# Windowed attention and a convolutional feed-forward on one core: weight decoding ahead of the convolution in steps 16 to 24

## The chip, the cores and the metric

One core of a Trainium2 chip runs the whole kernel. The metric is the device time of one execution in microseconds (us), 464.05 us as the median of 3 runs before the change (463.93 to 464.62). Each engine runs its own instructions strictly in order: TensorE (PE) multiplies, VectorE (DVE) and GpSimd (POOL) do elementwise work, ScalarE (ACT) does activations and copies, SyncE (SP) issues most transfers. They meet through semaphores.

## The reference

Attention over 4 batches, 8 heads, 768 positions, head width 64; a query sees 8 global keys and the 96 keys up to its own position, with a slope per head on the distance. Its output, 768 rows of 512 per batch, goes through a feed-forward block with double precision weights, of which the kernel gets the raw 64-bit words.

```python
scores = scale * q @ k.T + bias            # bias = -slope * distance, -1e9 outside the window
a = exp(scores - max(scores)); a = a / (sum(a) + 1e-9)
x = (a @ v) as (batch, 768, 512)
h = maximum(x @ w_in, 0)                   # 512 -> 1024
conv = sum over k in 0..2 of conv_w[k] * h shifted by k - 1 along the positions
out = (h * 1 / (1 + exp(-conv))) @ w_out   # 1024 -> 512
```

## The kernel before, in words

A job is a pair of heads over half a batch (384 queries): 32 jobs of 3 steps each, 96 steps of 128 queries. Step s runs `scores(s)` on TensorE (L385 for the first nine jobs, L395 later), `maxima(s)` on VectorE (L412, two instructions for two heads), `exps(s)` on ScalarE (L426), and, one or two steps late, the rest of the earlier steps: `normalise(s - 1)` takes the reciprocal of the row sums on VectorE (L438) and scales one head on GpSimd (L444) and one on ScalarE (L442); `transposes(s - 2)` (TensorE, L452) and `evict(s - 2)` (ScalarE, L457) turn the probabilities; at a job's end `values` multiplies by v (L473), and `mixed_high` (ScalarE, L485) and `mixed_low` (VectorE, L489) split the result into two float32r planes.

The feed-forward of one half batch (12 steps) is a queue of small items that `fill` works off between the steps of the next half batch. `mm1` multiplies by w_in in three parts for each of 8 blocks f (L507) and ends with a ReLU on ScalarE (L517), which also frees the PSUM bank; up to step 26 there is one such bank, so block f + 1 can't begin before the ReLU of block f. `conv` takes the middle tap on ScalarE (L555, later on GpSimd, L557) and the outer two on VectorE (L558, L559), both on what L555 wrote. For each pair of blocks follow a tanh on ScalarE (`gate`, L577) and a check for saturation (`saturated`, L588). `split` (L610, L612, L613) makes the gated planes and `mm2` multiplies by w_out (L622).

The weights must be made float32 planes. Piece by piece (16 of 128x512; w4_1 is piece 4, half 1), SP loads the words (L307), VectorE puts sign, exponent and mantissa together in three instructions (L316, L318, L320), GpSimd rounds to the high plane (L325), VectorE subtracts for the low one (L331). These wait as chores, and `work("dve", budget)` issues them, in their order, until the budget of its step is used up. A piece that is finished (L320) frees the load four pieces later.

From job 9 on (step 27) q and k are split too, into qh, ql, kk: GpSimd copies (L137, L138), VectorE subtracts (L141, L142), and kk's raw tile has one buffer, so its next load follows the subtraction.

The first 25 steps (s below `HAND`) are laid out by hand: each engine's instructions run in the order in which the program's lines issue them. From step 25 on a scheduler orders each engine's instructions by its own model of the time, starting from where the hand-laid part left the engines. So an edit to the hand-laid steps also changes orders behind them.

In a hand-laid step VectorE's part is: maxima(s), the reciprocal of step s - 1, at a job's end the split of its values, then what `fill` issues (the outer taps of a convolution, in five of the steps from 17 on: 17, 19, 20, 22, 23), then the chores.

Of the kernel before, what the change touches and what calls it, by code (L numbers as in the profile page):

```python
# [33 lines left out]
NU, SPU = 2 * B, NPAIR * NB  # L34
LAG_T, LAG_V = 2, 4
# [10 lines left out]
DECODE_BY_HAND, DECODE_LATER = (0.3, 1.2), (1.35,)  # L46
# [21 lines left out]
def fast_path(tc, io):  # L68
# [99 lines left out]
    def warm(n):  # L168
        for _ in range(n):
            T.matmul(wp[:, :P], wz, wz, start=True, stop=True)  # L170
# [52 lines left out]
    def table(h, c0=0, c1=NT, X=V):  # L223
        r = slice(c0, c1)
        if X is A:
            A.activation(tab[:, h, r], rel[:, r], AF.Copy, scale=-(2.0 ** (2 - h)))
            return
        X.tensor_scalar(tab[:, h, r], rel[:, r], -(2.0 ** (2 - h)), 1.0, ALU.mult, ALU.mult)
# [143 lines left out]
    def scores(s):  # L372
        m, i = steps[s]
        b, u, hp = jobs[m]
        w = NKC[u]
        first = u == 0 and i == 0
        n, c0 = (W0, NPREV) if first else (WIN, 0)
        k0 = key_start(u, i)
        both = ps_s.tile([P, 2, 256], F32, tag="s", name=f"s{s}")
        sp = [both[:, 0], bank(f"sb{s}", True) if m < BESIDE else both[:, 1]]  # L380
        for j in range(2):
            if m < NATIVE:
                rq, rk = raw[m]
                r, a = (j * D, 0) if m < BESIDE else (0, j)
                last_mm[s] = T.matmul(  # L385
                    sp[j][:, c0 : c0 + n],
                    rq[r : r + D, a * TB + i * P : a * TB + (i + 1) * P],
                    rk[r : r + D, a * w + k0 : a * w + k0 + n],
                    start=True,
                    stop=True,  # L390
                )
                continue
            qh, ql, kk = qk[m]
            for n_, (q_, st, sp_) in enumerate(((qh, True, False), (ql, False, True))):
                last_mm[s] = T.matmul(  # L395
                    sp[j][:, c0 : c0 + n],
                    q_[:, j * TB + i * P : j * TB + (i + 1) * P],
                    kk[:, j * w + k0 : j * w + k0 + n],
                    start=st,
                    stop=sp_,  # L400
                )
        st_s[s] = (sp, c0, n, first)
# [43 lines left out]
    def transposes(s):  # L446
        m, i = steps[s]
        pb, _, _, _ = st_s.pop(s)
        pt = ps_t.tile([P, 2, 2, P], F32, tag="t", name=f"t{s}")
        for j in range(2):  # L450
            for c in range(2):
                T.transpose(pt[:, j, c, :], pb[:, j, c * P : (c + 1) * P], ident)  # L452
        st_pt[s] = pt
# [6 lines left out]
    def values(m):  # L460
        pv[m] = ps_v.tile([P, TB], F32, tag="v", name=f"pv{m}")
        with contextlib.ExitStack() as es:
            if "auto" in cur:
                es.enter_context(tc.high_priority())
                es.enter_context(tc.manual_schedule(engines={mybir.EngineType.PE}))
            for i in (NB - 1, *range(NB - 1)):
                block(m, i)
# [23 lines left out]
    def ends(s):  # L491
        return s >= 0 and s % NB == NB - 1
# [218 lines left out]
    def check_some(cost):  # L711
        pace[0] += cost
        while pace[1] < NCHK and pace[0] >= CHECK_EVERY * (pace[1] + 1):
            check_piece(pace[1])
            pace[1] += 1
    last_exp, last_mm, last_ev = {}, {}, {}

    def share(s):
        e = s - LAG_V - 1
        if e < 0:  # L720
            return 0
        if e % SPU == SPU - 1:
            queue.extend(ffn(e // SPU))
        left = SPU - (e + 1) % SPU + 1
        if e + 1 >= len(steps) - SPU:
            left += 1
        return -(-sum(cost for cost, _, _ in queue) // left)

    def fill(k):
        with contextlib.ExitStack() as es:  # L730
            if "auto" in cur:
                p, e = cur["s"] - 1, cur["s"] - LAG_T - 1
                if cur["s"] > len(steps) and e in last_ev:
                    es.enter_context(tc.issue_after(last_ev[e].ins))
                for last in (last_ttr, last_exp, last_mm):
                    if p in last:
                        es.enter_context(tc.issue_after(last[p].ins))
            while queue and (k > 0 or queue[0][0] == 0):
                cost, fn, a = queue.pop(0)
                fn(*a)  # L740
                k -= cost
                if words:
                    check_some(cost)
# [5 lines left out]
    def work(eng, budget):  # L749
        q = chores[eng]  # L750
        credit[eng] = min(credit[eng], 0.0) + budget
        while q and credit[eng] > 0 and q[0][0] <= cur["s"]:
            _, cost, fn, args = q.pop(0)
            fn(*args)
            credit[eng] -= cost
# [40 lines left out]
    for s in range(len(steps) + LAG_V + 1):  # L796
        cur["s"] = s
        m, i = steps[s] if s < len(steps) else (len(jobs), -1)
        if s < HAND:
            scores(s)  # L800
            if ends(s - LAG_V):
                values((s - LAG_V) // NB)
            if s < len(WARM_INSIDE):
                warm(WARM_INSIDE[s])
            x = (s - LAG_V - 1) // NB if ends(s - LAG_V - 1) else None
            k = share(s)
            k0 = 0 if x is not None else k // 2
            fill(k0)
            if s >= LAG_T:
                transposes(s - LAG_T)  # L810
            if x is not None:
                mixed_high(x)
            maxima(s)
            exps(s)
            if s >= LAG_T:
                evict(s - LAG_T)
            if s:
                normalise(s - 1)
            if x is not None:
                mixed_low(x)  # L820
            if i == 1 and m + 1 < NPAIR:
                table(2 * m + 2, X=G)
                table(2 * m + 3, X=G)
            fill(k - k0)
            if s < LAG_V + SPU:
                mm1_early(s)
            if s + 1 < len(WARM):
                warm(WARM[s + 1])
            if s == 0:
                load_conv_weights()  # L830
            if s == 5:
                limits()
            if s in (4, 6):
                conv_weights((s - 4) // 2)
            budget = DECODE_BY_HAND[min(s // 3, len(DECODE_BY_HAND) - 1)]
            work("dve", budget if s < LAG_V + SPU else DECODE_LATER[0])
            work("pool", 1.3)
        else:
            if hand:
                hand = False  # L840
                cur["auto"] = True
                manual.__exit__(None, None, None)
            if s < len(steps):
                scores(s)
                maxima(s)
                exps(s)
            k = share(s)
            e = s - LAG_V - 1
            if ends(e):
                mixed_high(e // NB)  # L850
                mixed_low(e // NB)
            if s <= len(steps):
                normalise(s - 1)
            if s < LAG_V + SPU:
                mm1_early(s)
            k0 = int(k * SHARE[e % 2])
            fill(k0)
            if ends(s - LAG_V):
                values((s - LAG_V) // NB)
            if s < len(steps) + LAG_T:  # L860
                transposes(s - LAG_T)
                evict(s - LAG_T)
            fill(k - k0)
            if s < len(steps):
                budget = DECODE_LATER[min((s - HAND) // 3, len(DECODE_LATER) - 1)]
                with tc.issue_after(last_ttr[s].ins):
                    work("dve", budget)
                    work("pool", 1.2)
        if s == len(steps):
            for k in range(3):  # L870
                check_load()
        if s == 0:
            for k in range(len(order)):
                chain(*order[k])
        elif s == 1:
            load_v(0)
            load(2)
        for k, at in enumerate(FIRST_LOADS):
            if at == s:
                start_piece(k)  # L880
        if i == 0:
            prep(m + 1, 0)
            prep(m + 1, 1)
            if 1 <= m < NATIVE - 2:
                load(m + 2)
        elif i == 1 and m + 2 >= NATIVE:
            load(m + 2)
        if s >= NB and i == 0:
            load_v(m)
# [186 lines left out]
```

## Time and profile before

| what | value |
|---|---|
| median of 3 runs | 464.05 us |
| the profiled execution | 464.1 us |
| its span, first to last instruction | 462.3 us |
| mean granted TensorE clock | 0.977 |
| busy: PE | 436.2 us (94%) |
| busy: DVE | 359.2 us (78%) |
| busy: ACT | 311.2 us (67%) |
| busy: POOL | 221.1 us (48%) |
| chain that ended last | PE 70%, DVE 18%, ACT 8% |

The profiled execution lasted 1.8 us longer than its span. The shares are means over stages with different limits: the rows below are cut by stage. Step s is told by its maxima: those of step 17 stand at 47.91 us, of 18 at 54.62, of 24 at 83.10.

### The profile page before, as it was taken

Reading aid. Unit: us, or ns where it says so; the run is one execution under the profiler, and the core shown is the slowest. Engines: PE = TensorE matmul, PEld = TensorE weight load, DVE = VectorE, ACT = ScalarE, POOL = GpSimd, SP = SyncE. Lnnn points to the kernel's source line nnn. Section 1 sums busy time; section 2 is a strip of 40 time slices with the busy share of each in tenths; the row PEclk is TensorE's granted clock in tenths of the full one; section 3 lists DMA queues with packets and bytes.
Section 4 is the critical chain, followed back from the end, with each engine's and each line's share of the span. In section 5 each row is a group of like instructions: output and inputs, shape, how many; then the busy total and the mean of one; then the engine's idle time right before and its main releaser. Section 6 shows DMA issues by size and latency. Waiting matters only on the chain.

```text
span 462.3 us, 9052 instructions
## 1 busy us (share of the span) xinstructions
PE 436.2 (94%) x3039; PEld 377.9 (82%) x3039; DVE 359.2 (78%) x935; ACT 311.2 (67%) x839; POOL 221.1 (48%) x307
## 2 busy tenths in 40 slices
PE   7888878589999999999999999999999999999997
PEld 6665656478888898889988998889988998799876
DVE  6889766999899899776799889767799987468700
ACT  4879667766988667555678677645668686755440
POOL 5545211544436766555675685555766743013000
PEclk9989998868999999999999999999999999999999
DMA  7897546024432423444224422443334322891111
GB/s 212 274 269 196 151 117 202 29 72 130 167 103 79 159 77 102 150 128 137 85 87 137 158 72 84 128 138 126 115 112 113 130 81 70 279 308 74 45 47 52
DMA packets 22662, 60.02 MB, mean 130 GB/s; under 512 B 3024, under 2 KB 5584, under 8 KB 22608
## 3 DMA queue, kind: packets, MB, share of 16 engines
q1 hardware_dynamic: 18992, 53.01, 37.8%
q10 hardware_dynamic: 3616, 6.36, 3.8%
q8 instruction: 26, 0.43, 0.4%
q14 instruction: 28, 0.23, 0.2%
HBM read 53.07 MB, written 6.29 MB: 128 GB/s over the span
## 4 chain that ended last, share of the span: by engine, by line
PE 70%; DVE 18%; ACT 8%; issue 2%; POOL 1%; DMA 1%; ACTq 0%; DVEq 0%; POOLq 0%
PE o L622 26%; PE h L507 24%; PE pv L473 7%; PE t L452 6%; PE s L395 6%; ACT pbuf L426 3%; DVE s L412 2%; DVE c L558 2%; DVE w L318 2%; DVE w L320 1%; ACT pt L457 1%; DVE gl L613 1%; DVE c L559 1%; PE last L643 1%; DVE kk L141 1%
## 5 line engine op out<-in xcount | busy, mean ns | idle before, releaser
L444 POOL TENSOR_SCALAR pbuf<-pbuf,mm 128x232 f32<-128x232 f32 (+1 forms) x160 | 115.0, 728 | 92.5 <-DVE mm L438 60.3
L426 ACT ACTIVATE pbuf<-s,mm 128x232 f32<-128x232 f32 (+1 forms) x165 | 71.7, 440 | 56.5 <-DVE mm L412 46.8
L412 DVE CUSTOM_DVE_ANT_0 s<-s,tab 128x232 f32<-128x232 f32 (+1 forms) x165 | 63.1, 385 | 22.3 <-PE s L395 15.6
L452 PE MATMUL t<-ident,pbuf 128*128 128x128 f32 x384 | 66.2, 283 | 9.7 <-ACT pbuf L442 4.6
L622 PE MATMUL o<-woh,gh 128*128 128x512 f32 x184 | 74.3, 404 | 0.0
L622 PE MATMUL o<-wol,gh 128*128 128x512 f32 x184 | 73.4, 399 | 0.0
L622 PE MATMUL o<-woh,gl 128*128 128x512 f32 x184 | 73.2, 399 | 0.0
L452 PEld LDWEIGHTS t<-ident,pbuf 128*128 128x128 f32 x384 | 47.4, 144 | 23.7 <-ACT pbuf L442 8.5
L507 PE MATMUL h<-xh,wih 128*128 128x384 f32 x252 | 60.5, 353 | 4.6 <-ACT hbuf L517 3.1
L457 ACT ACTIVATE pt<-t 128x512 f32<-128x512 f32 x96 | 56.9, 595 | 9.6 <-PE t L452 7.9
L557 POOL TENSOR_SCALAR c<-hbuf,cw 128x382 f32<-128x382 f32 (+1 forms) x48 | 37.2, 778 | 54.2 <-ACT hbuf L517 54.2
L507 PE MATMUL h<-xl,wih 128*128 128x384 f32 x252 | 60.6, 349 | 0.2 <-DVE xl L489 0.2
L558 DVE SCALAR_TENSOR_TENSOR c<-hbuf,cw,c 128x382 f32<-128x382 f32 (+1 forms) x64 | 45.2, 714 | 17.3 <-ACT c L555 11.6
L507 PE MATMUL h<-xh,wil 128*128 128x384 f32 x252 | 56.4, 346 | 0.0
L507 PEld LDWEIGHTS h<-xh,wih 128*128 128x128 f32 x252 | 44.1, 194 | 8.3 <-ACT hbuf L517 5.7
L473 PE MATMUL pv<-pt,v 128*64 128x128 f32 (+1 forms) x768 | 50.0, 279 | 0.1
L473 PEld LDWEIGHTS pv<-pt,v 128*64 128x64 f32 (+1 forms) x768 | 42.3, 138 | 8.1 <-issue 2.9
L507 PEld LDWEIGHTS h<-xh,wil 128*128 128x128 f32 x252 | 44.8, 192 | 0.7 <-issue 0.7
L507 PEld LDWEIGHTS h<-xl,wih 128*128 128x128 f32 x252 | 44.1, 191 | 0.9 <-issue 0.5
L559 DVE SCALAR_TENSOR_TENSOR c<-hbuf,cw,c 128x382 f32<-128x382 f32 (+1 forms) x64 | 43.3, 678 | 0.6
L395 PE MATMUL s<-kk,qh 128*128 128x232 f32 (+1 forms) x138 | 36.7, 291 | 6.2 <-DVE kk L141 5.3
L517 ACT ACTIVATE hbuf<-h 128x384 f32<-128x384 f32 x64 | 30.9, 491 | 16.5 <-PE h L507 16.4
(120 smaller groups left out, 854.8 us busy)
## 6 DMA issues: line engine op xcount, KB each, us to landing
v<-in_vv SPq DMA_DIRECT2D x32, 384.0 KB, 3.4
rq<-in_qk SPq DMA_DIRECT2D x23, 384.0 KB, 3.1
wr<-in_w SPq DMA_DIRECT2D x16, 512.0 KB, 4.6
check<-in_w SPq DMA_DIRECT2D x16, 512.0 KB, 4.7
rk<-in_qk SPq DMA_DIRECT2D x12, 504.0 KB, 3.6
out<-ob ACTq DMA_DIRECT2D x23, 256.0 KB, 2.3
rk<-in_qk SPq DMA_DIRECT2D x11, 408.0 KB, 3.7
rq<-in_qk SPq DMA_DIRECT2D x16, 96.0 KB, 5.0
```

The lines of the kernel that those rows point to most:

```text
L395: last_mm[s] = T.matmul(sp[j][:, c0 : c0 + n], q_[:, j * TB + i * P : j * TB + (i + 1) * P], kk[:, j * w + k0 : j * w + k0 + n], start=st, ...
L412: last_ttr[s] = V.tensor_tensor_reduce(out=sp[j][:, c0 : c0 + n], in0=sp[j][:, c0 : c0 + n], in1=tb, scale=-0.125, scalar=3.0e38, op0=ALU. ...
L426: last_exp[s] = A.activation(pb[:, j, c0 : c0 + n], sp[j][:, c0 : c0 + n], AF.Exp, bias=mm[:, j : j + 1], scale=-1.0, accum_out=mm[:, 2 + ...
L444: G.tensor_scalar(x, x, inv, 1.0, ALU.mult, ALU.mult)
L452: T.transpose(pt[:, j, c, :], pb[:, j, c * P : (c + 1) * P], ident)
L457: last_ev[s] = A.activation(sb, st_pt[s], AF.Copy)
L473: T.matmul(pv[m][64 * j : 64 * j + 64, i * P : (i + 1) * P], vt[m][:n, i, c, 64 * j : 64 * j + 64], sb[:n, j, c, :], start=c == 0, stop=c ...
L507: T.matmul(ps[:, :TB], w_[:, k, fs], x_, start=part == 0 and k == 0, stop=part == 2 and k == NK - 1,)
L557: G.tensor_scalar(c, *tap(1), 1.0, ALU.mult, ALU.mult)
L558: V.scalar_tensor_tensor(c, *tap(0), c, ALU.mult, ALU.add)
L559: V.scalar_tensor_tensor(c, *tap(2), c, ALU.mult, ALU.add)
L622: last = T.matmul(ps, g_[:, f], w_[:, f], start=f == 0 and part == 0, stop=f == NF - 1 and part == 2,)
```

## The change

In steps 16 to 24 (`LAG_V + SPU` is 16) the call that issues VectorE's decoding chores moves from behind the second `fill` to ahead of it. Which chores are issued in a step stays the same, and so does everything before step 16. GpSimd's call stays where it was.

```diff
+            budget = DECODE_BY_HAND[min(s // 3, len(DECODE_BY_HAND) - 1)]
+            if s >= LAG_V + SPU:
+                work("dve", DECODE_LATER[0])
             fill(k - k0)
             if s < LAG_V + SPU:
                 mm1_early(s)
...
             if s in (4, 6):
                 conv_weights((s - 4) // 2)
-            budget = DECODE_BY_HAND[min(s // 3, len(DECODE_BY_HAND) - 1)]
-            work("dve", budget if s < LAG_V + SPU else DECODE_LATER[0])
+            if s < LAG_V + SPU:
+                work("dve", budget)
             work("pool", 1.3)
```

On VectorE in step 17 (- before, + after the change; the c tile is the convolution's, w4_0, w3_1 and w4_1 are pieces of weights, mm16 holds step 16's sums, s18 step 18's scores):

```order
 L438 RECIPROCAL mm16_814<-mm16_814 128x2
-L558 SCALAR_TENSOR_TENSOR c0_864<-hbuf_190,cw_185,c0_864 128x382
-L559 SCALAR_TENSOR_TENSOR c0_864<-hbuf_190,cw_185,c0_864 128x382
 L320 SCALAR_TENSOR_TENSOR w4_0_791<-wr4_0_620,w4_0_791 128x512
 L331 TENSOR_TENSOR wil_187<-w3_1_748,wih_186 128x512
-L316 TENSOR_SCALAR w4_1_872<-wr4_1_648 128x512
+L316 TENSOR_SCALAR w4_1_864<-wr4_1_648 128x512
+L558 SCALAR_TENSOR_TENSOR c0_870<-hbuf_190,cw_185,c0_870 128x382
+L559 SCALAR_TENSOR_TENSOR c0_870<-hbuf_190,cw_185,c0_870 128x382
 L412 ISA s18_875,mm18_902<-s18_875,tab_166 128x232
```

The same three chores now stand between the reciprocal and the two taps; steps 19, 20, 22 and 23 change alike, with two or three chores each.

On VectorE behind step 25's maxima, up to the subtraction for job 9's keys (kk9), which step 27's scores need. Before the change:

```order
L318 SCALAR_TENSOR_TENSOR w7_0_1241<-wr7_0_1006,w7_0_1241 128x512
L331 TENSOR_TENSOR wol_189<-w6_0_1101,woh_188 128x512
L438 RECIPROCAL mm24_1172<-mm24_1172 128x2
L320 SCALAR_TENSOR_TENSOR w6_1_1189<-wr6_1_920,w6_1_1189 128x512
L559 SCALAR_TENSOR_TENSOR c0_864<-hbuf_190,cw_185,c0_864 128x382
L320 SCALAR_TENSOR_TENSOR w7_0_1241<-wr7_0_1006,w7_0_1241 128x512
L438 RECIPROCAL mm25_1206<-mm25_1206 128x2
L141 TENSOR_TENSOR kk9_1194<-rk9_1104,kk9_1194 64x816
```

And after it:

```order
L412 ISA sb26_1249,mm26_1252<-sb26_1249,tab_166 128x232
L412 ISA mm26_1252 128x1
L318 SCALAR_TENSOR_TENSOR w7_0_1241<-wr7_0_999,w7_0_1241 128x512
L559 SCALAR_TENSOR_TENSOR c0_870<-hbuf_190,cw_185,c0_870 128x382
L141 TENSOR_TENSOR kk9_1194<-rk9_1104,kk9_1194 64x816
L438 RECIPROCAL mm25_1206<-mm25_1206 128x2
L320 SCALAR_TENSOR_TENSOR w7_0_1241<-wr7_0_999,w7_0_1241 128x512
```

Step 25's reciprocal and piece w7_0's last instruction moved behind kk9; the other instructions of the stretch stand in another order ahead of it.

On ScalarE around the last tanh of the first half batch, L577 (the exponentials of step 29 read s29; xh7 is job 7's high plane):

```order
 L432 ACTIVATE mm28_1338<-mm28_1338,misc_181 128x2
-L426 ACTIVATE pbuf2_195,mm29_1395<-s29_1390,mm29_1395 128x232
+L577 ACTIVATE c0_870<-c0_870 128x2x382
+L442 ACTIVATE pbuf1_194<-pbuf1_194,mm28_1338 128x232
 L457 ACTIVATE pt25_1311<-t25_1306 128x512
-L426 ACTIVATE pbuf2_195,mm29_1395<-s29_1390,mm29_1395 128x232
-L577 ACTIVATE c0_864<-c0_864 128x2x382
 L457 ACTIVATE pt26_1371<-t26_1366 128x512
 L485 ACTIVATE xh7_1344<-pv7_1290 128x384
+L426 ACTIVATE pbuf2_195,mm29_1395<-s29_1390,mm29_1395 128x232 x2
```

The tanh moved ahead of step 29's exponentials, and these behind job 7's high plane.

## Rows read from the trace of the kernel before

**Rows 1.** Windows: stretch, length, busy PE, PEld, DVE, ACT, POOL; PEclk, DMA share, GB/s.
```profile
48.47:83.55 35.08, 29.51 (x205) 22.45 (x206) 23.13 (x66) 23.74 (x67) 6.60 (x12) 0.95 0.51 146
83.55:117.05 33.50, 24.69 (x158) 22.20 (x156) 32.12 (x70) 23.82 (x68) 15.95 (x18) 0.80 0.28 87
92.70:100.00 7.30, 6.97 (x28) 6.58 (x29) 7.00 (x17) 4.38 (x12) 4.21 (x5) 0.52 0.38 111
117.05:462.30 345.25, 341.45 (x2306) 303.71 (x2306) 263.89 (x656) 226.50 (x581) 173.37 (x220) 1.00 0.37 117
```
**Rows 2.** Waits of PE, 117.05 to 440: us in total, times, longest.
```profile
PE h L507 <- ACT hbuf L517: 0.9, 1, 0.9
```
**Rows 3.** Chain that ended last, step 17 into 18: start us, us, what.
```profile
51.47 0.63 DVE c L558
...
52.12 0.62 DVE c L559
52.74 0.60 DVE w L320
...
54.69 0.32 DVE s L412
```
**Rows 4.** Waits, 48.47 to 83.55.
```profile
DVE c L558 <- ACT c L555: 11.6, 5, 2.7
```
**Rows 5.** DVE timeline, steps 19 to 24: start us, us, instruction, [idle before <-releaser].
```profile
60.30 0.62 DVE L558 SCALAR_TENSOR_TENSOR c<-hbuf,cw,c 128x382 f32<-128x382 f32 x1 [2.01 <-ACT c L555]
...
74.60 0.62 DVE L558 SCALAR_TENSOR_TENSOR c<-hbuf,cw,c 128x382 f32<-128x382 f32 x1 [1.97 <-ACT c L555]
...
81.90 0.69 DVE L331 TENSOR_TENSOR wol<-w,woh 128x512 fp32r<-128x512 f32 x1
...
83.10 0.30 DVE L412 CUSTOM_DVE_ANT_0 s<-s,tab 128x136 f32<-128x136 f32 x1
```
**Rows 6.** ACT timeline, steps 17 to 24.
```profile
53.62 0.49 ACT L517 ACTIVATE hbuf<-h 128x384 f32<-128x384 f32 x1 [2.19 <-PE h L507]
55.16 0.45 ACT L426 ACTIVATE pbuf<-s,mm 128x232 f32<-128x232 f32 x1 [1.05 <-DVE mm L412]
...
57.60 0.45 ACT L426 ACTIVATE pbuf<-s,mm 128x232 f32<-128x232 f32 x1
...
59.67 0.60 ACT L555 ACTIVATE c<-hbuf,cw 128x382 f32<-128x382 f32 x1
60.17 0.47 ACT L517 ACTIVATE hbuf<-h 128x384 f32<-128x384 f32 x1
61.61 0.84 ACT L577 ACTIVATE c<-c 128x764 f32<-128x764 f32 x1 [0.96 <-DVE c L559]
63.58 0.45 ACT L426 ACTIVATE pbuf<-s,mm 128x232 f32<-128x232 f32 x1 [1.13 <-DVE mm L412]
...
66.16 0.47 ACT L517 ACTIVATE hbuf<-h 128x384 f32<-128x384 f32 x1
...
67.36 0.19 ACT L588 ACTIVATION_READ_ACCUMULATOR sat<-c,misc 128x1 f32 x1
69.23 0.45 ACT L426 ACTIVATE pbuf<-s,mm 128x232 f32<-128x232 f32 x1 [1.68 <-DVE mm L412]
...
83.55 0.37 ACT L426 ACTIVATE pbuf<-s,mm 128x136 f32<-128x136 f32 x1 [1.59 <-DVE mm L412]
```
**Rows 7.** PE timeline, steps 20, 21 and 27.
```profile
60.70 0.96 PE L507 MATMUL h<-xh,wih 128*128 128x384 f32 x4 [0.89 <-ACT hbuf L517]
...
64.80 0.97 PE L507 MATMUL h<-xh,wil 128*128 128x384 f32 x4
...
92.71 0.75 PE L395 MATMUL s<-kk,qh 128*128 128x136 f32 x2 [5.30 <-DVE kk L141]
```
**Rows 8.** POOL timeline, steps 18 and 19.
```profile
55.64 0.72 POOL L444 TENSOR_SCALAR pbuf<-pbuf,mm 128x232 f32<-128x232 f32 x1 [1.23 <-DVE mm L438]
...
57.82 0.46 POOL L444 TENSOR_SCALAR pbuf<-pbuf,mm 128x232 f32<-128x232 f32 x1 [0.25 <-PE t L452]
```

## The prediction

> **What bounds the kernel now.** I read the windows by stage first, because the shares of the whole span hide that the kernel has two regimes. From 117.05 us to the end TensorE is busy 341.45 of 345.25 us at the full 2.4 GHz, and its longest wait on another engine there, up to 440 us, is 0.9 us: work taken off another engine in that stretch buys nothing [rows 1, 2]. Ahead of it TensorE is not the limit: it is busy 29.51 of 35.08 us from step 17's exponentials to step 24's (48.47 to 83.55), and 24.69 of 33.50 from there to 117.05, where VectorE is busy 32.12, or 96% [rows 1]. The order of the work behind 117.05 needs the same matmuls whenever it starts. So what the change is worth is by how much earlier this last stretch begins.
>
> Second, the chain of waits in step 17. It runs from VectorE's two taps (51.47 and 52.12) through the decoding (from 52.74) into step 18's maxima at 54.69 [rows 3]. So the decoding lies on the path, between taps and maxima. Third, the waits: VectorE stood idle 11.6 us in this stretch, five times, ahead of L558, for the middle tap on ScalarE, which comes late in ScalarE's step [rows 4]. The shortest of the five is 1.97 us [rows 5]. The same engine idles ahead of the convolution and then lets everybody wait for chores behind it.
>
> **The change in steps 17 to 24.** No instruction is added or dropped. In five steps the chores go from behind the taps into that idle time. What they take on the path, from the end of L559 to the next maxima, is 54.69 - 52.74 = 1.95 us in step 17 [rows 3] and 83.10 - 81.90 = 1.20 in step 23 [rows 5]; with the three steps between them 7.5 us for the five. Each is below the idle time of its step, so VectorE alone would give back all 7.5. Not all of it arrives, since ScalarE and TensorE come next. I walk from one step's exponentials to the next, L426 on ScalarE.
>
> Without chores a step with a convolution takes 2.07 us from the exponentials to the middle tap (57.60 to 59.67), 0.63 from there to L558 (60.30), 0.65 to L559, 0.62 to the maxima, and some 0.5 more to the exponentials (54.69 to 55.16): 4.4 us [rows 3, 5, 6].
>
> - 17 to 18: now 6.69 us (48.47 to 55.16). ScalarE has a ReLU ahead of step 18's exponentials, at 53.62, which waited 2.19 us for TensorE and doesn't move [rows 6]. The exponentials can start when it is through, about 54.0: 5.5 us instead of 6.7.
> - 18 to 19: 2.44 us (55.16 to 57.60), filled by ScalarE's own work, with no wait at its end. It stays.
> - 19 to 20: now 5.98 us. The tanh L577 stands ahead of step 20's exponentials and waits for L559 (61.61, after 0.96 idle) [rows 6]. 2.07 + 0.63 + 0.65 + 0.65 to the tanh, and 0.75 for it: 4.75 us.
> - 20 to 21: now 5.65. A ReLU and the saturation check stand ahead, 1.39 us from the ReLU's start at 66.16 to the check's end (67.36 + 0.19) [rows 6]. The ReLU needs block 3 of mm1, which TensorE begins when the ReLU of block 2 is done (60.70, after 0.89 idle) and ends at 64.80 + 0.9, 5.0 us later [rows 7]. With everything 1.2 earlier by then it ends at 64.5; 64.5 + 1.4 = 65.9, against exponentials of step 20 at 61.2: 4.7 us.
> - 21 to 24: now 14.32 us (69.23 to 83.55) [rows 6]. The three steps repeat those above: one without a convolution, 2.45; one with a tanh, 4.75; one with a ReLU and a check, block 5's, 4.5. That is 11.7.
>
> The sum is 5.5 + 2.44 + 4.75 + 4.7 + 11.7 = 29.1 us where 35.08 stood: 6.0 us, and 1.5 of VectorE's 7.5 stay with ScalarE and TensorE. TensorE itself gains less: 1.2 us at block 3, 1.7 at its ReLU (66.16 to 64.5), and by the same walk about 4.0 at step 25's scores, since its waits for ReLUs stay.
>
> The chores must find their inputs when they are called earlier. GpSimd's rounding follows L320 in the same step and L331 comes one step or more later, and a load follows the piece four before it; all of these move with the chores. I cost this at nothing; were one late by more than what is left of the idle time, the taps queued behind it would be late by the rest.
>
> **From step 24 to 117.** VectorE's list up to the first `split` holds the same work in another order, and it is 96% busy, so a start 6.0 us earlier carries through. Two details help: kk9 has one L320 and one reciprocal less ahead of it (0.7 us by the 0.60 of rows 3 and a small reciprocal), and the tanh comes ahead of step 29's exponentials, so `split` waits less. TensorE's wait of 5.30 us for kk9 [rows 7] shrinks by the 2 us by which VectorE gains more than TensorE. The later transfers of k follow kk's subtractions and move along. I take these details at zero in the sum, minus 1.5 us as their best end and plus 2 as the worst, because the scheduler's orders differ from here on and no row shows them. From 117.05 on: no change.
>
> So 464.1 - 6.0 = 458.1 us against the profiled execution's own time, which agrees with the median of the runs (464.05).
>
> Something speaks against the new place. Behind the reciprocal GpSimd scales a head (L444): beside VectorE's decoding it took 0.72 us, and alone 0.46 [rows 8]. The Trainium skill ("SBUF — State Buffer", section "SBUF: two separate sides") says that the two share one pair of ports, which one of them holds for a whole instruction. The rows agree in direction, with 0.26 us. By it each of the five moves would make L444 or one chore later by at most an L444, 0.46 us; the rest of the idle time covers this in four steps, and in step 22 about 0.2 would show: 458.3 instead of 458.1.
>
> **Rivals.**
> - *Only TensorE's own gain arrives.* If between 83.55 and 117.05 the matmuls decide rather than VectorE, the 4.0 us by which TensorE reaches step 25's scores earlier are what counts: 460.1; with the scheduler's order worth 2 us less, 462. For it: the granted clock there is 0.80, so TensorE has less in hand than its 24.69 busy us say. Against it: its 5.30 us wait for VectorE [rows 1, 7].
> - *More arrives.* After that wait TensorE ran from 92.70 to 100.00 at a granted 0.52, that is nearly all at 1.2 GHz [rows 1], so its work took about 3.5 us more than at 2.4. If the shorter wait keeps the higher clock, and the details above come in, 2 to 3.5 us are added: 455.5. Against it: VectorE, not TensorE, carries the chain here. The Trainium skill ("TensorE: Matmul & The Clock Gate", section "HAM oscillation — how this bites in real kernels") says that idle stretches throw TensorE back to the lower clock; the row agrees, with 0.52 behind 5.30 us idle.
> - *Slower.* The scheduler starts from another state, and its new orders from step 25 on could make TensorE wait in its full stretch, where it waited hardly at all. The place is steps 30 to 36: there VectorE does convolution, splits and maxima and has next to no idle time. The price of one such wait is that for kk9, 5.30 us: one gives 463.4, no change to speak of; two give 464.1 - 6.0 + 10.6 = 468.7. It decides from 6.0 us of new waiting on. Against it: the scheduler kept these waits at 0.9 us before [rows 2], and it starts with VectorE further ahead of TensorE.
> - *It does nothing*: if the taps, and not the chores, were what the next maxima waited for. The chain shows both in line [rows 3], so hardly.
>
> **How the numbers follow.** The forecast, 458.1 with its own range 456.6 to 459.8 (the details' best end, and most of their worst), has 0.53; TensorE's own gain (459.8 to 462.8) 0.21; more (below 456.6) 0.14; no gain, with the one new wait, 0.04; slower 0.08. From 455.4 to 462.6 the range leaves out a tail of the larger gain (0.04), no gain and slower (0.12), and a little of the second case. A measurement of this kernel tells 0.2% from no change, 0.9 us: faster 0.88, same 0.04, slower 0.08.
>
> **What would show it.** The wait of L558 for the middle tap should fall from 11.6 to some 3 us over the five steps. Step 24's exponentials should stand near 77.6 us, the scores that wait for kk9 near 86, with a wait of 2 to 3 us, and TensorE should be full from about 111. It is wrong if L558 still idles as long, if a chore waits for a load, if step 24's exponentials stand later than 79.5, or if TensorE shows waits of over 2 us behind 115.

## The result, and the profile after

The changed kernel takes 457.38 us as the median of 4 runs (456.88 to 460.29), beside 464.24 for the kernel before on the same chip: ratio 0.9865, 95% interval 0.9829 to 0.9901. A second measurement of the same kernel (the first experiment below) gave 456.49, ratio 0.9846 (0.9812 to 0.988). The forecast was 458.1, so a gain of 6.0 us was expected and 6.9 to 7.8 came.

The profiled execution of the changed kernel happened to be the longest of the four: 460.29 us, span 458.4. It was already late before the first changed instruction. The windows of the two kernels from 20 to 40 us, where their instructions are the same, show why (columns as in [rows 1]; the granted clock is the third number from the end). Before the change:

```profile
20.00:30.00 10.00, 8.41 (x71) 6.10 (x69) 8.32 (x31) 8.11 (x29) 5.59 (x8) 0.83 0.84 253
30.00:40.00 10.00, 8.36 (x69) 5.04 (x65) 9.16 (x31) 8.72 (x31) 4.20 (x6) 1.00 0.84 221
```

And after it:

```profile
20.00:30.00 10.00, 8.42 (x63) 6.18 (x61) 8.25 (x31) 7.58 (x27) 5.59 (x8) 0.73 0.83 255
30.00:40.00 10.00, 8.43 (x68) 5.45 (x67) 7.83 (x28) 7.82 (x25) 3.74 (x5) 0.93 0.63 173
```

TensorE is as busy, but it stays longer at its lower level (1.2 GHz) and completes fewer matmuls (63 against 71). Step 17's exponentials stand at 49.95 us instead of 48.47; the difference arises between 27 and 32 us, where the same matmuls take longer (the 24 of `values`, for one, 2.83 us instead of 2.24). So I read the profile after by distances from step 17, and use the second profile of the same kernel (span 455.2, step 17 at 48.57) for what stands against [rows 1].

The walk of ScalarE's exponentials (L426), ReLUs and tanhs through steps 17 to 24, after the change, answers to [rows 6]:

```profile
49.95 0.45 ACT L426 ACTIVATE pbuf<-s,mm 128x232 f32<-128x232 f32 x1
55.10 0.49 ACT L517 ACTIVATE hbuf<-h 128x384 f32<-128x384 f32 x1 [2.19 <-PE h L507]
55.49 0.45 ACT L426 ACTIVATE pbuf<-s,mm 128x232 f32<-128x232 f32 x1
57.92 0.45 ACT L426 ACTIVATE pbuf<-s,mm 128x232 f32<-128x232 f32 x1
61.92 0.84 ACT L577 ACTIVATE c<-c 128x764 f32<-128x764 f32 x1 [0.96 <-DVE c L559]
62.67 0.43 ACT L426 ACTIVATE pbuf<-s,mm 128x232 f32<-128x232 f32 x1
66.12 0.49 ACT L517 ACTIVATE hbuf<-h 128x384 f32<-128x384 f32 x1 [0.80 <-PE h L507]
67.43 0.44 ACT L426 ACTIVATE pbuf<-s,mm 128x232 f32<-128x232 f32 x1
```

None of these exponentials waits for VectorE's maxima any more (in [rows 6] four of them show 1.05 to 1.68 us). Each stands right behind ScalarE's own work: in steps 18, 20, 21, 23 and 24 a ReLU, a tanh or a check, which wait for TensorE or for the taps, and in steps 19 and 22, which follow a step without a convolution, the high plane of a job (L485). The chain that ended last, in the same step as [rows 3] (start us, us, what), has left VectorE:

```profile
50.00 0.97 PE h L507 x4
...
52.70 1.47 PE pv L473 x24
54.17 0.91 PE h L507 x4
...
55.10 0.02 ACT hbuf L517
...
55.49 0.54 ACT pbuf L426 x2
```

VectorE's idle time ahead of the taps, 49.95 to 79.20, against the 11.6 us of [rows 4], with what is now its only other wait (us in total, times, longest; `s` and `sb` are the scores of the two heads):

```profile
DVE c L558 <- ACT c L555: 4.8, 5, 1.5
DVE s L412 <- PE sb L385: 0.8, 1, 0.8
```

And the windows that answer to [rows 1], of the second profile, whose step 17 stands where it stood before: the hand-laid steps 17 to 24, then up to 108 us, the stretch behind job 9's first scores, and the rest.

```profile
48.57:77.86 29.29, 25.98 (x198) 20.08 (x199) 23.35 (x69) 23.34 (x67) 9.11 (x13) 1.00 0.55 171
77.86:108.00 30.14, 24.48 (x154) 21.45 (x153) 29.62 (x65) 23.45 (x69) 13.34 (x16) 0.83 0.26 83
85.89:93.00 7.11, 5.60 (x22) 5.11 (x23) 6.80 (x18) 4.06 (x12) 4.65 (x5) 0.53 0.39 114
108.00:455.20 347.20, 342.60 (x2317) 304.09 (x2316) 269.53 (x658) 226.61 (x582) 171.62 (x220) 1.00 0.36 118
```

The starts of the same pieces of work in the three profiles, in us:

| | before | after | after, second profile | second - before |
|---|---|---|---|---|
| exponentials of step 17 (L426) | 48.47 | 49.95 | 48.57 | +0.1 |
| exponentials of step 24 | 83.55 | 79.20 | 77.86 | -5.7 |
| first scores of job 9 (L395) | 92.71 | 87.24 | 85.89 | -6.8 |
| first mm2 (L622) | 131.8 | 125.0 | 124.0 | -7.8 |
| span | 462.3 | 458.4 | 455.2 | -7.1 |

The gain is made in steps 17 to 24 and carried to the end. VectorE stays 98% busy up to 108 us (29.62 of 30.14).

### The profile page after: what moved, and what is told of

Its sections match the earlier page's. It is cut to its first block, busy times and chain, and to the rows that moved or that the text cites. A ratio compares the mean times of both kernels' runs of the same rounds, so it can differ in the third digit from the quotient of the medians.

```text
span 458.4 us, 9062 instructions
## 1 busy us (share of the span) xinstructions
PE 435.3 (95%) x3039; PEld 375.4 (82%) x3039; DVE 362.5 (79%) x935; ACT 310.0 (68%) x839; POOL 219.9 (48%) x307
## 4 chain that ended last, share of the span: by engine, by line
PE 64%; DVE 17%; ACT 10%; DMA 5%; issue 3%; POOL 1%; DVEq 0%; ACTq 0%; SPq 0%; POOLq 0%
PE o L622 23%; PE h L507 19%; PE pv L473 7%; PE t L452 6%; PE s L395 5%; DMA check<-in_w 5%; ACT pbuf L426 3%; DVE s L412 2%; DVE c L558 2%; ACT pt L457 2%; DVE gl L613 1%; DVE c L559 1%; PE last L643 1%; DVE ql L142 1%; DVE hbuf L610 1%
## 5 line engine op out<-in xcount | busy, mean ns | idle before, releaser
L444 POOL TENSOR_SCALAR pbuf<-pbuf,mm 128x232 f32<-128x232 f32 (+1 forms) x160 | 113.1, 717 | 107.8 <-DVE mm L438 57.4
L426 ACT ACTIVATE pbuf<-s,mm 128x232 f32<-128x232 f32 (+1 forms) x165 | 71.5, 440 | 56.0 <-DVE mm L412 37.5
L622 PE MATMUL o<-woh,gh 128*128 128x512 f32 x184 | 74.5, 405 | 0.3 <-ACT hbuf L517 0.3
L622 PE MATMUL o<-wol,gh 128*128 128x512 f32 x184 | 73.6, 400 | 0.0
L622 PE MATMUL o<-woh,gl 128*128 128x512 f32 x184 | 73.0, 398 | 0.0
L507 PE MATMUL h<-xh,wih 128*128 128x384 f32 x252 | 60.8, 351 | 3.0 <-ACT hbuf L517 2.4
L507 PE MATMUL h<-xl,wih 128*128 128x384 f32 x252 | 59.2, 344 | 1.1 <-DVE xl L489 1.1
L507 PE MATMUL h<-xh,wil 128*128 128x384 f32 x252 | 56.0, 343 | 0.0
L558 DVE SCALAR_TENSOR_TENSOR c<-hbuf,cw,c 128x382 f32<-128x382 f32 (+1 forms) x64 | 45.1, 712 | 10.0 <-ACT c L555 5.1
L507 PEld LDWEIGHTS h<-xh,wih 128*128 128x128 f32 x252 | 43.6, 191 | 6.6 <-ACT hbuf L517 5.1
L507 PEld LDWEIGHTS h<-xl,wih 128*128 128x128 f32 x252 | 43.5, 189 | 1.9 <-DVE xl L489 1.4
L507 PEld LDWEIGHTS h<-xh,wil 128*128 128x128 f32 x252 | 44.3, 191 | 0.5 <-issue 0.5
L622 PEld LDWEIGHTS o<-woh,gl 128*128 128x128 f32 x184 | 34.6, 188 | 7.5
```

The lines of the kernel that those rows point to most:

```text
L426: last_exp[s] = A.activation(pb[:, j, c0 : c0 + n], sp[j][:, c0 : c0 + n], AF.Exp, bias=mm[:, j : j + 1], scale=-1.0, accum_out=mm[:, 2 + ...
L444: G.tensor_scalar(x, x, inv, 1.0, ALU.mult, ALU.mult)
L507: T.matmul(ps[:, :TB], w_[:, k, fs], x_, start=part == 0 and k == 0, stop=part == 2 and k == NK - 1,)
L558: V.scalar_tensor_tensor(c, *tap(0), c, ALU.mult, ALU.add)
L622: last = T.matmul(ps, g_[:, f], w_[:, f], start=f == 0 and part == 0, stop=f == NF - 1 and part == 2,)
```

## The experiments

All were timed in five rounds; each ratio is to the kernel before on the same chip, with its 95% interval.

**The same kernel again.**

> The changed kernel once more. Theory: the profile on record was 1.5 us late at step 10 already, at instructions that did not change, so a typical execution takes 456.9 to 458, step 17's exponentials stand near 48.5 us and step 24's near 77.7. Rival (the late start belongs to the new code): step 17's exponentials stand near 50 again and the time is near 460.

456.49 us, 0.9846 (0.9812 to 0.988), a little below the range given. Step 17 stands at 48.57 us, so the 1.5 us at step 17 belong to the execution and not to the change. The walk to step 24 has the same length in both profiles, 29.29 and 29.25 us.

**Only one half of the steps.** The first kernel moves the call in steps 16 to 20, the second in 21 to 24.

```diff
+            if LAG_V + SPU <= s <= 20:      # first half;  second half: if s > 20:
+                work("dve", DECODE_LATER[0])
             fill(k - k0)
```

> Chores ahead of the convolution in steps 16 to 20 only. Theory (the idle time ahead of L558 is what is gained, step by step): the hand-laid steps gain 1.2 + 1.2 + 0.95 = 3.4 us by step 21's exponentials (65.9 from 69.2) and nothing in the steps behind; time 460 to 461.5, half of the whole change. Rival (the new order of the scheduled part is the gain): no relation to the number of steps moved; about 457.4 or about 464.

460.24 us, 0.9912 (0.9877 to 0.9947).

> Chores ahead of the convolution in steps 21 to 24 only. Theory: steps 22 and 23 gain 1.4 + 1.0 us, plus 0.2 in step 21, 2.6 us by step 24's exponentials; time 461 to 462.5, and the gains of the two halves sum to that of the whole within 1.5 us. Rival (scheduled part): about 457.4 or about 464, and the two halves don't sum.

460.12 us, 0.9918 (0.9887 to 0.995). The walk takes 31.52 us with the first half and 32.90 with the second, that is 3.56 and 2.18 less than the 35.08 of [rows 1], in sum 5.74 beside 5.79 for both together. So the hand-laid steps add up step by step, as in the walk. The times add up within the noise as well: 4.1 and 4.2 us, in sum 8.3, beside 7.8 for the whole. But a half's time is not its walk: the second half gains 4.2 us, of which 2.18 lie in the walk; the rest lies behind step 24, where the orders differ too. With the first half TensorE's wait for job 9's keys is still 5.31 us, with the second 1.76; and the second pays a part back further on:

```profile
PE s L395 <- ACT pbuf L426: 2.2, 2, 2.0
PE s L395 <- DVE kk L141: 1.8, 1, 1.8
PE s L395 <- DVE ql L142: 1.1, 1, 1.1
```

These are TensorE's longest waits behind 76 us in the second half's profile (us in total, times, longest); the first of them holds 1.97 us at 127.21, in a stretch where the kernel before waits 0.9 at most [rows 2].

**The scheduler's order alone.** The kernel before, with another budget behind step 25, so that the scheduled part is laid anew and the hand-laid part is untouched:

```diff
-                budget = DECODE_LATER[min((s - HAND) // 3, len(DECODE_LATER) - 1)]
+                budget = 1.2
```

> The kernel before with nothing changed in the hand-laid steps, and a decoding budget of 1.2 instead of 1.35 in the scheduled steps from 25 on, so that only the scheduler's orders differ. Theory: these orders are worth little, 464.2 within 1.5 us either way, with step 24's exponentials at 83.5. Rival (the new orders are the gain): the time moves by 3 us or more, down or up.

463.29 us, 0.9975 (0.9953 to 0.9998): a new order was worth about 1 us here, and the walk stayed (step 24 at 83.45). So the 5.8 us of the walk, where the scheduler orders nothing, are no accident of its order. This run can't say the same of the 1 to 2 us that the change gains behind step 24: one other order was tried, and it moved the time by as much.

**The gap closed in another way.** The convolution's middle tap (L555) right behind its ReLU on ScalarE in the hand-laid steps; the decoding stays behind the taps.

```diff
+        if n == 0 and not exact and cur["s"] < HAND:
+            early_tap(n, f)
...
+        A.activation(
+            cbuf[n][:, f, :w], hbuf[:, f, t0 + 1 : t1 + 1], AF.Copy,
+            scale=cw[:, NF + f : NF + f + 1],
+        )
```

> The kernel before, with its chores behind the convolution, but in the hand-laid steps the middle tap on ScalarE stands right behind the ReLU of its block instead of a step later, so that L558 finds it ready. Theory (what the change used is VectorE's idle time ahead of L558; any way of closing that gap is worth as much): the wait of L558 for the tap falls from 11.6 us to under 1.5 in the five steps, step 17's to step 24's exponentials take 28.5 to 30 us instead of 35.1, and the time is 457 to 459.5. Rival (the place of the chores, or the order of the scheduled part, matters, not the gap): 462 to 464.5.

455.09 us, 0.9812 (0.9786 to 0.9838), below the range expected. The walk takes 29.64 us, 0.35 more than with the change. (Counted from step 16's exponentials, where the early tap already costs ScalarE 0.5 us, it is 32.74 beside 31.84, and 37.63 before.) It meets the same bound, three ReLUs that wait for TensorE:

```profile
53.47 0.49 ACT L517 ACTIVATE hbuf<-h 128x384 f32<-128x384 f32 x1 [2.43 <-PE h L507]
64.62 0.49 ACT L517 ACTIVATE hbuf<-h 128x384 f32<-128x384 f32 x1 [1.63 <-PE h L507]
76.56 0.49 ACT L517 ACTIVATE hbuf<-h 128x384 f32<-128x384 f32 x1 [1.37 <-PE h L507]
```

No chore was moved, and the walk falls by nearly as much: in the hand-laid steps the gain comes from closing that idle time, whichever way it is closed. The rest of the gain lies behind step 24: TensorE waits 1.34 us for job 9's keys instead of 5.30 [rows 7]. The scheduler's orders are new there as well, and what they are worth was not tried apart.

**Both.** The change and the early tap.

> The changed kernel, and the middle tap early as well. Theory: the gap can be closed once only; what is left in these steps is set by ScalarE and by TensorE's ReLUs, and the tap moves ahead of the exponentials of steps 18, 21 and 24, where it costs 0.5 us each. So 0 to 2 us come on top: 455 to 457. Rival (two gains that add up): another 5 us, 451 to 452.

450.57 us, 0.9718 (0.9696 to 0.974), the fastest kernel here. The time is the one that I had as the rival, but not for its reason: the walk is no shorter (29.64 us), so the two gains don't add up there. My theory was right on the hand-laid steps and wrong on the end. VectorE, with no wait for a tap left, gets through two chores more in the walk (21 against 19), and the scheduler lays the subtraction of job 9's keys ahead of a chore, a tap and step 26's maxima that stood ahead of it with the change alone. So it starts at 81.20 us instead of 84.74. The scores of job 9 then come without a wait, and TensorE's granted clock, 0.52 and 0.53 behind these scores before and after the change, stays at 1.00. Windows of the two, change alone first:

```profile
77.86:120.00 42.14, 36.48 (x246) 32.93 (x245) 40.96 (x90) 33.67 (x95) 18.75 (x22) 0.88 0.32 104
```

```profile
78.54:120.00 41.46, 37.18 (x275) 33.27 (x274) 40.28 (x88) 34.45 (x99) 21.95 (x22) 1.00 0.35 113
```

TensorE is busy about as long and completes 275 matmuls instead of 246. Over the span its busy time falls from 433.7 to 430.0 us for the same matmuls, which I put down to the clock, and its idle time from 21.5 to 19.5; the two make up the 5.7 us between the spans (455.2 and 449.5). How much of this the chores bring and how much the new order was not tried apart.

The stretch from 88 to 92 us in three kernels, with the change, with the early tap and with both:

```profile
88.00:92.00 4.00, 3.40 (x13) 3.41 (x14) 3.69 (x11) 1.70 (x7) 1.96 (x3) 0.50 0.40 123
88.00:92.00 4.00, 4.00 (x27) 3.65 (x27) 4.00 (x12) 2.16 (x9) 2.70 (x3) 0.64 0.20 75
88.00:92.00 4.00, 3.12 (x36) 2.61 (x36) 3.97 (x12) 3.59 (x12) 2.06 (x3) 1.00 0.00 2
```

The length of one wait doesn't tell these apart: ahead of the second row TensorE's waits are 1.34 and 1.11 us, and ahead of the third one is 1.53 us.

**More chores.** The change, with a larger budget in three steps, where VectorE still waited for a tap.

```diff
-                work("dve", DECODE_LATER[0])
+                work("dve", DECODE_LATER[0] + (0.62 if s in (17, 20, 23) else 0))
```

> The changed kernel with a larger budget in steps 17, 20 and 23 (1.97 instead of 1.35), so that three more chores fit into what idle time is left there (1.0, 1.5 and 1.5 us). Theory (behind step 24 VectorE sets the pace): three chores of 0.6 us leave that stretch, kk9 comes 1.5 to 2 us earlier counted from step 24's exponentials, and the time is 454.5 to 455.5. Rival (TensorE's own work sets the pace there): 456 to 457.

454.1 us, 0.9796 (0.9772 to 0.9819). The walk stays at 29.25 us with three chores more in it, and VectorE is busy 25.18 us of it instead of 23.35. So about 2 us of the idle time that the change leaves could still be used. From step 24's exponentials to the end this profile takes some 2 us less than the second profile of the change (375.2 and 377.3 us), so they came back. They didn't come by way of job 9's keys, as I had expected: their subtraction starts 6.79 us behind these exponentials, where 6.88 stood.

**Job 9's split one step earlier.** First with the change, then in the kernel before.

```diff
+        if s == 3 * (NATIVE - 1) - 1:
+            prep(NATIVE, 0)
+            prep(NATIVE, 1)
```

> The changed kernel with job 9's k and q split (L137, L138, L141, L142) a step earlier, ahead of step 24's maxima, so that TensorE's wait of 2.7 us for kk9 and of 1.5 for ql9 goes. VectorE's work up to the first split is the same. Theory (VectorE sets the pace behind step 24, and TensorE's waits there cost nothing by themselves): 456.5 within 1 us; step 24's exponentials 2.2 us later. Rival (these waits are the path): 453 to 454.5.

455.61 us, 0.9837 (0.9814 to 0.986). The wait for the keys is gone, and the walk is 2.4 us longer (31.65): step 24's exponentials now wait 2.32 us for maxima that stand behind the split. The time is within the range expected. Against the change it is 0.4 to 1.3 us less by the ratios, inside their intervals, so it isn't shown that taking the wait away won anything.

> The kernel before with job 9's split of q and k one step earlier and no other edit: TensorE's wait of 5.30 us for kk goes, the decoding stays behind the convolution. Theory on the clock: a part of what the change gives comes from TensorE's granted clock behind that gap (0.5 to 0.7 from 88 to 100 us before the change, 0.5 for about half as long with it, 1.00 throughout where the gap is gone), so the kernel gains 2.5 to 4 us: 460 to 461.5 us. Rival: VectorE is what is late, the wait only names its place, and the earlier split delays step 24's maxima by as much; the lower clock falls on a TensorE that would wait anyway: 463 to 464.5 us.

462.35 us, 0.9978 (0.9956 to 1.0): between the two. TensorE's waits behind 76 us (us in total, times, longest) show where the 5.30 us went:

```profile
PE s L385 <- ACT pbuf L426: 3.2, 1, 3.2
PE s L395 <- ACT pbuf L426: 2.8, 1, 2.8
PE h L507 <- DVE xl L489: 1.4, 1, 1.4
```

The wait only changed its name: VectorE is what is late there, as the rival said. The walk is 39.18 us, 4.1 more than before, and step 24's exponentials show why:

```profile
86.22 0.37 ACT L426 ACTIVATE pbuf<-s,mm 128x136 f32<-128x136 f32 x1 [5.25 <-DVE mm L412]
```

My theory on the clock falls in this form, because the clock fell behind the new waits as well (0.60 from 88 to 92 us, 0.70 from 100 to 104). Of the kernels here only the one with change and early tap keeps it at 1.00 from 76 to 120 us.

**All together.** Change, early tap and larger budget; then job 9's earlier split as well.

> The change, the earlier middle tap and the larger budget of chores in steps 17, 20 and 23 together. Theory: in the kernel with change and tap TensorE still waits 1.5 us for VectorE's ql behind step 24 and about 5 us in all up to 160 us, so VectorE is still late there, and chores taken out of that stretch come back about in full: 448.5 to 449.7 us (1 to 2 us below the 450.6 of change and tap). Rival: with the tap early VectorE has no waits left in the hand-laid steps that a larger budget could fill, so the extra chores lengthen the walk as much as they relieve later: 450 to 451.5 us.

455.5 us, 0.9814 (0.9783 to 0.9846), 5 us above the kernel without the larger budget. Both expectations missed. The walk is 29.68 us, as long as without it. Behind step 24 TensorE waits anew:

```profile
PE s L395 <- DVE kk L141: 2.3, 1, 2.3
PE t L452 <- POOL pbuf L444: 1.6, 3, 1.0
PE t L452 <- ACT pbuf L442: 0.7, 1, 0.7
PE s L395 <- DVE ql L142: 0.7, 1, 0.7
```

The scheduler starts from another state and lays kk9 later again (5.92 us behind step 24's exponentials, 2.66 without the larger budget), and GpSimd's scalings too late for the transposes at 139 to 142 us. Over the span TensorE idles 22.8 us instead of 19.5, and its clock is 0.81 and 0.77 from 84 to 92 us. That the scheduler's orders made the difference is read from these rows; it was not tried apart.

> The same, with job 9's split of q and k one step earlier. Theory: TensorE's wait for kk of job 9 is already gone with the early tap, and the earlier split stands ahead of step 24's maxima, so nothing is won and up to 2 us is lost: 449 to 451.5 us. Rival: what is left behind step 24 is the wait for ql of job 9 (1.5 us), which this takes away: 447 to 448.5 us.

453.15 us, 0.9761 (0.973 to 0.9791): the wait for the keys is gone again, and TensorE waits 1.3 to 1.5 us each for exponentials in three places. Neither expectation held, since both were reckoned from what the kernel above was expected to take.

## Why the prediction was right, point by point

- **The walk.** 29.1 us was predicted, 29.25 and 29.29 came. Step by step after the change: 5.54, 2.43, 4.75, 4.76, and 11.77 from 21 to 24 (5.5, 2.44, 4.75, 4.7 and 11.7 predicted). Of VectorE's 7.5 us ScalarE and TensorE were to keep 1.5, and they keep 1.7: the ReLU of step 17 still waits 2.19 us for TensorE, and the chain runs over L507.
- **The idle time ahead of L558** fell from 11.6 to 4.8 us where some 3 was given. With the walk 5.8 us shorter and as much work, VectorE's idle time had to fall by about 6, not by the 7.5 of its chores; the 3 was inconsistent with my own sum.
- **TensorE's own gain** by step 25's scores: 4.0 predicted; they stand at 76.67 us in the second profile and at 80.23 before, 3.6.
- **The stretch behind step 24** carried the gain, as VectorE's 96% there said. The rival in which only TensorE's own gain arrives fell: job 9's scores come 6.8 us earlier, not 4.
- **The details at zero** are the term that was mis-sized. In the second profile 1.1 us came by job 9's scores, whose wait for kk9 is inside the 2 to 3 us predicted, and 1.0 more by the first mm2. Behind that 0.7 went back, in a stretch with a new wait for VectorE's xl (L489):

```profile
85.89 0.46 PE L395 MATMUL s<-kk,qh 128*128 128x136 f32 x2 [2.71 <-DVE kk L141]
...
148.99 0.45 PE L507 MATMUL h<-xl,wih 128*128 128x384 f32 x1 [1.07 <-DVE xl L489]
```

Net -1.4, near the best end given (-1.5). The prediction had named the gain at kk9; that the orders behind it took no more than 0.7 us back is luck as far as it goes, since it had no row for them.

- **The clock** did not bring it as the rival had it. Behind job 9's scores TensorE ran 7.11 us at a granted 0.53, where 7.30 us at 0.52 stood in [rows 1], although the wait was half as long. For 84 to 88 us the second profile shows TensorE busy 1.20 of 4 us, so the wait ahead of the scores is not all of its idle time. The Trainium skill ("TensorE: Matmul & The Clock Gate", section "HAM oscillation — how this bites in real kernels") says that gaps in TensorE's work bring the lower clock; the rows agree, with 0.53 behind the wait of 2.71 us and around one of 1.50. The fastest kernel keeps 1.00 from 78.54 to 120 us with waits of up to 1.53 us.
- **Slower**: its place was steps 30 to 36, its price two waits of 5.3 us. The waits that came behind 115 us are 1.07 us in the second profile and four of 0.3 to 1.1 us in the first. The sign of that rival holds as a risk: the all-together kernel lost 5 us, in part to such waits.
- **GpSimd beside the chores.** The prediction read 0.26 us more for L444 from [rows 8] and took at most an L444, 0.46 us, as the delay of either side. In steps 17, 20 and 23 it takes 1.23 to 1.26 us, where 0.46 stood; first GpSimd's row of step 17 after the change, then VectorE's:

```profile
50.41 1.26 POOL L444 TENSOR_SCALAR pbuf<-pbuf,mm 128x232 f32<-128x232 f32 x1 [2.35 <-DVE mm L438]
```

```profile
50.15 0.67 DVE L320 SCALAR_TENSOR_TENSOR w<-wr,w 128x512 int32<-128x512 int32 x1
50.74 0.68 DVE L331 TENSOR_TENSOR wil<-w,wih 128x512 fp32r<-128x512 f32 x1
51.34 0.60 DVE L316 TENSOR_SCALAR w<-wr 128x512 int32<-128x512 int32 x1
52.95 0.62 DVE L558 SCALAR_TENSOR_TENSOR c<-hbuf,cw,c 128x382 f32<-128x382 f32 x1 [1.00 <-ACT c L555]
```

L444 ends at 51.67 us, 0.33 behind the start of L316, and VectorE's chores keep their length. It looks as if L444 waits until the two chores with two inputs are through and then runs beside the third. The Trainium skill ("SBUF — State Buffer", section "SBUF: two separate sides") says that one of the two engines holds the shared ports for a whole instruction while the other is blocked; the rows agree in direction, with GpSimd as the one that waits. By that rule an L444 was the wrong bound for GpSimd's side: it waits for a chore, which is longer. L444 takes 0.77 to 0.80 us more here, and one chore 0.67. The delay cost next to nothing: TensorE's transposes wait 0.3 us for L444 in all of steps 17 to 24.

## What to carry to other kernels

Where an engine idles ahead of an instruction and the others then wait for chores behind it, move the chores into the idle time, and walk the next bound of each step to see how much arrives: here 6.0 of 7.5 us, and the chip gave 5.8 in these steps. The engine that is nearly full behind the changed stretch says whether the gain is carried on. Where a scheduler lays out what follows, an edit that helps on top of one kernel can cost time on top of another (the larger budget won about 2 us with the change and lost 5 with the early tap as well), so each combination has to be measured.

## What was not expected of the hardware

- The first 50 us, with the same instructions, differ between executions by how long TensorE stays at its lower clock. Step 17's exponentials stand at 49.95 us with a granted 0.73 and 0.93 from 20 to 40 us, at 48.47 with 0.83 and 1.00, and at 47.06 with 1.00 throughout (the kernel with more chores): a spread of 2.9 us that no edit made. Two profiles are best lined up at the last unchanged instruction.
- TensorE's busy time is no measure of its work: 436.2 us before, 433.7 in the second profile and 430.0 in the fastest kernel, for the same matmuls.
